# Attention, three-way MoE and squared-ReLU MoE on one core: conversion of the weights and block 1's attention listed later within block 0, and other places for block 1's keys and values

## The chip, the core and the metric

The program runs on 1 core of one Trainium2 chip. The metric is the time of one execution on the device in microseconds (us). The kernel before took 1547.14 us in the median of 3 runs (1546.5 to 1547.54).

The core's engines run side by side, each through its own list of instructions in a fixed order: PE (matmul), DVE (vector), ACT (activation), POOL (GpSimd), and SP, which here only issues DMAs. An instruction that waits holds up everything behind it on its engine.

## The reference

All inputs are float32. With B = 8 batches, H = 8 heads, S = 576 positions and D = 64, so 4608 tokens of width 512:

```
k_p, v_p = mean of k, v over groups of 8 positions        # 72 keys and values per head
attn = softmax(q @ k_p.T / sqrt(D))                       # row maximum subtracted
x = (attn @ v_p), heads side by side                      # 4608 x 512
h = max(x @ w1, x @ w2, x @ w3)                           # 4608 x 768
y = h @ w_out                                             # 4608 x 512
g = max(y @ w_in, 0);  out = (g * g) @ w_out2             # 768 and 2048 hidden columns
```

## The kernel before

**Numbers.** A float32 operand is split into a high and a low part, and each product is made of three matmuls (`PARTS`). The weights arrive as 64-bit numbers in 512 KB pieces and are converted on the chip. One conversion (`weights`, lines 128 to 164) is one DMA on SP into a tile `wraw`, two ACT instructions (L148, L149), two DVE instructions (L150, L153), the high part on ACT (`w` or `wo` from `wbits`, L121) and the low part on POOL (L122). The first stage needs 24 of them: `w_f_e` for f = 0 to 5 and e = 0 to 2, and `wo_0` to `wo_5`.

**Blocks.** The tokens go through attention and the first MoE in 12 blocks of 384 (`moe1`). Block 0 is the first 384 tokens of batch 0. Block 1 is the last 192 tokens of batch 0 and the first 192 of batch 1, so it is the first that needs the keys and values of batch 1. A block's MoE has 22 steps (`STEPS`): 18 that make `h` (one for each weight piece `w_f_e`, 12 matmuls at L465) and 4 that make `y` (18 matmuls each at L484). Attention of a block is done for four pairs of heads: load, prepare (pooled keys `ks` into `kbd`, the queries' parts `qs`), scores and softmax (`sc`, `st`, `ss`), transpose (`tr`, `pt`), values (`av`, then the pair's part of `x`, split by ACT at L121 and DVE at L122). Every matmul of a step reads all four pairs' `x`. So the steps of f = 0 begin pair by pair as `x` comes, and the steps of f = 1 start only when the fourth pair is there. Below, x0 to x3 are the four pairs of block 0.

**What sets the order.** `todo` is a list of pieces of work with a listing time in steps; `run` sorts it and calls the pieces, and a scheduler then places each instruction on its engine, in an order of its own that starts from this one. Block j's steps are listed from 22 j on; block 1's attention is listed from about ten steps before block 0's first step on; conversion i (0 to 23) is listed at 0.9 i - 12 (lines 505 to 508).

**Places.** The raw tiles of this stage (`wraw`, the keys `kr`, the values `vr`) take four places in turn (`place`). Six tiles `spare0` to `spare5` have the places in which `wo_0` to `wo_5` are kept later; until then block 0's own loads use them once: `kq` (keys and queries of a pair, four tiles) and `natural` (three tiles, the values of batch 0, pooled by matmuls `vp` at L250). These are seven loads, so the last `kq` takes one of the four raw places. All DMAs that matter here are issued by SP, in its order.

Of the kernel before, what the change touches and what calls it, by code (L numbers as in the profile page):

```python
# [10 lines left out]
F32 = mybir.dt.float32  # L11
# [9 lines left out]
P = 128  # L21
B, H, S, D = 8, 8, 576, 64
POOL = 8
SP = S // POOL
NPAIR = H // 2
NT = B * S
DM = H * D
KD = DM // P
FF1 = 768
KF1 = FF1 // P  # L30
FF2 = 2048
KF2 = FF2 // P
NE = 3
# [11 lines left out]
STEPS = NE * KF1 + KD  # L45

LEAD_LOAD, LEAD_PREP, LAG_T, LAG_V, LEAD_X = 10, 4, 3, 3, 4

# [32 lines left out]
def attention_moe_kernel(ctx: ExitStack, tc: tile.TileContext, q, k, v, vn, w1, w2, w3, wo1, wi2, wo2, out):  # L85
# [27 lines left out]
    def place(kind):  # L113
        if shared[0]:
            turns["both"] += 1
            return f"raw{turns['both'] % 4}"
        turns[kind] += 1
        return f"raw{2 * kind + turns[kind] % 2}"
# [56 lines left out]
    raw_p = s_at.enter_context(tc.tile_pool(name="raw_p", bufs=4, side="right"))  # L175
# [23 lines left out]


    spare = [f"spare{i}" for i in range(KF1)]
    unused = list(spare)

    def early(shape, name):
        if unused:
            return w_p.tile(shape, F32, tag=unused.pop(0), name=name)
        return raw_p.tile(shape, F32, tag=place(1), name=name, bufs=1)

    def load_k(b, p):
        kr = raw_p.tile([P, 2 * 512], F32, tag=place(1), name="kr", bufs=1)[:, :S]  # L210
        nc.sync.dma_start(out=kr, in_=k[b, p])
        return kr

    def load_v(b, p):
        vr = raw_p.tile([P, 2, D, POOL], F32, tag=place(1), name="vr", bufs=1)[:SP]
        nc.sync.dma_start(out=vr, in_=v[b - NATURAL, :, 2 * p : 2 * p + 2])
        return vr

# [12 lines left out]
    def load_natural(b):  # L231

        tiles = []
        for s0 in range(0, S, 2 * P):
            t = early([P, 2, DM], "natural") if b == 0 else raw_p.tile([P, 2, DM], F32, tag=place(1), name="natural", bufs=1)
            n = min(2 * P, S - s0)
            if n == 2 * P:
                nc.sync.dma_start(out=t, in_=vn[b, s0 : s0 + n].rearrange("(a p) d -> p a d", p=P))
            else:
                nc.sync.dma_start(out=t[:n, 0], in_=vn[b, s0 : s0 + n])  # L240
            tiles.append(t)
        return tiles

    def pool_v(tiles):
        vp = mm_ps.tile([P, 512], F32, tag="ps", name="vp")[:SP]
        last = (S - 1) // P
        for i in range(last + 1):
            n = min(P, S - i * P)
            c = MID - i * P // POOL
            nc.tensor.matmul(  # L250
                vp, lhsT=sums[:n, c : c + SP], rhs=tiles[i // 2][:n, i % 2], start=(i == 0), stop=(i == last)
            )
        for h in range(2):
            vh = vp.rearrange("s (p h d) -> s h p d", h=2, d=D)[:, h]
            split_scaled(vst[:, :, 2 * h], vst[:, :, 3 + 2 * h], vh, V_SCALE)
# [3 lines left out]
    def pieces(j):  # L259

        t = 0
        while t < T1:
            b, s0 = divmod(j * T1 + t, S)
            n = min(T1 - t, S - s0)
            yield b, s0, n, t
            t += n

    def score_tiles(n):
        m = P if n % P == 0 else n // 2
        return [(c, m) for c in range(0, n, m)]  # L270

    def attention(j):

        x_t[j] = [None] * NPAIR
        n_tiles = sum(NPAIR * len(score_tiles(n)) for _, _, n, _ in pieces(j))
        pace = (STEPS - 1) / n_tiles
        at = (j - 1) * STEPS + pace / 2 - (LAG_T + LAG_V + LEAD_X)
        for b, s0, n, t in pieces(j):
            if s0 == 0 and b < NATURAL:
                tiles = []  # L280
                when = at - pace / 2 + LAG_T + LAG_V if t else at + pace / 2
                todo.append((when - LEAD_LOAD, lambda b=b, tiles=tiles: tiles.extend(load_natural(b))))
                todo.append((when, lambda tiles=tiles: pool_v(tiles)))
            for p in range(NPAIR):
                load, prepare, softmax, transpose, values = attend(j, b, s0, n, p, t)
                todo.append((at - LEAD_LOAD, load))
                todo.append((at - LEAD_PREP, prepare))
                tiles = score_tiles(n)
                if j < LIGHT:
                    todo.append((at, functools.partial(softmax, tiles)))  # L290
                for c, m in tiles:
                    if j >= LIGHT:
                        todo.append((at, functools.partial(softmax, [(c, m)])))
                    todo.append((at + LAG_T, functools.partial(transpose, c, m)))
                    at += pace
                todo.append((at - pace + LAG_T + LAG_V, values))

    used = []

# [7 lines left out]
    def attend(j, b, s0, n, p, t):  # L307
# [4 lines left out]
        def load():  # L312
            if j == 0:
                kq = early([P, 2 * 512], "kq")
                kr.append(kq[:, :S])
                qr.append(kq[:, S : S + n])
                nc.sync.dma_start(out=kr[0], in_=k[b, p])
            elif first:
                kr.append(load_k(b, p))
            if j:  # L320
                qr.append(raw_p.tile([P, T1], F32, tag="qr", name="qr", bufs=2)[:, :n])
            nc.sync.dma_start(out=qr[0], in_=q[b, p, :, s0 : s0 + n])
            if first and b >= NATURAL:
                vr.append(load_v(b, p))
# [177 lines left out]

    todo = []
    attention(0)
    for f in range(KF1):
        for e in range(NE):
            todo.append((0.9 * (NE * f + e) - 12, functools.partial(load_w1, f, e)))
    for kk in range(KF1):
        todo.append((0.9 * (NE * KF1 + kk) - 12, functools.partial(load_wo1, kk)))
    for j in range(NB1 - 1):  # L510
        add_moe1(j)
        attention(j + 1)
# [10 lines left out]
    for i, (src, raw, prepare) in enumerate(second):  # L523
        when = STEPS * (SECOND[0] + (i + 0.5) * (SECOND[1] - SECOND[0]) / len(second))
# [53 lines left out]
    early = [functools.partial(load_y, 0, r) for r in range(2)] + [functools.partial(mix_y, 0)]  # L578
# [150 lines left out]
```

## Time and profile before

| | us |
|---|---|
| median of 3 runs | 1547.14 |
| the profiled execution | 1546.39 |
| its span | 1544.7 |
| PE busy | 1509.4 |
| DVE busy | 948.2 |
| ACT busy | 623.5 |
| POOL busy | 199.4 |

The profiled execution took 1546.39 us, and its span, from the first to the last recorded instruction, is 1544.7 us. PE is busy for 98% of it. The page cuts the span into 40 slices; only in the first three is PE's busy share below nine tenths, and only in the first two is the granted clock at 7 tenths. So the rows of the profile that follow look at the first 127 us, in which block 0 is done.

### The profile page before, as it was taken

The numbers are of one execution on the slowest core, as the hardware profiler recorded it, in microseconds if no ns is written. First come the engines' busy times: TensorE is split into PE (matmuls) and PEld (weight loads), VectorE is DVE, ScalarE is ACT, GpSimd is POOL, SyncE is SP. The second block draws the span as 40 slices with busy tenths as digits, with TensorE's granted clock in tenths as the row PEclk, the third lists the DMA queues.
The fourth block names the chain that finished last, engine by engine and source line by source line (L and its number), as shares of the span: only waits on it lengthen the run. The fifth ranks groups of instructions, "written<-read, shape, count | busy, mean of one in ns | idle before, by whom it ended". The sixth has DMA issues, their size and how long they took to land.

```text
span 1544.7 us, 25098 instructions
## 1 busy us (share of the span) xinstructions
PE 1509.4 (98%) x9290; PEld 1413.8 (92%) x9290; DVE 948.2 (61%) x1991; ACT 623.5 (40%) x1772; POOL 199.4 (13%) x303
## 2 busy tenths in 40 slices
PE   6899999999999999999999999999999999999998
PEld 4789999999999999999999898988989888999987
DVE  6895678776776767755427555455655546464544
ACT  7875566656666556654212212121212112121211
POOL 5541122222222121322000000000000000000000
PEclk7799999999999999999999999999999999999999
DMA  7552234434334332323475424333333433343331
GB/s 226 159 172 68 76 105 149 145 95 143 122 119 143 97 132 99 102 77 123 135 289 208 150 109 164 110 121 123 112 137 124 150 123 108 111 150 109 137 109 69
DMA packets 80858, 200.87 MB, mean 130 GB/s; under 512 B 9024, under 2 KB 32576, under 8 KB 80736
## 3 DMA queue, kind: packets, MB, share of 16 engines
q1 hardware_dynamic: 73824, 189.83, 36.1%
q10 hardware_dynamic: 6912, 9.44, 1.7%
q8 instruction: 74, 1.21, 0.3%
q14 instruction: 48, 0.39, 0.1%
HBM read 157.29 MB, written 41.94 MB: 129 GB/s over the span
## 4 chain that ended last, share of the span: by engine, by line
PE 85%; DVE 5%; DMA 5%; ACT 2%; issue 2%; SPq 0%; POOL 0%; DVEq 0%; ACTq 0%; POOLq 0%
PE ps L465 25%; PE acc L645 25%; PE ps L600 21%; PE ps L484 9%; PE sc L344 2%; DMA out_dram<-o 2%; PE tr L370 2%; DMA wraw<-in_w_dram 1%; PE av L396 1%; PE av L395 1%; DVE wbits L153 1%; DMA vr<-in_v_dram 1%; DMA wraw<-in_wo_dram 1%; DMA kq<-in_k_dram 1%; DVE wbits L150 0%
## 5 line engine op out<-in xcount | busy, mean ns | idle before, releaser
L465 PE MATMUL ps<-x,w 128*128 128x384 f32 x2592 | 507.6, 343 | 1.8 <-DVE x L122 1.0
L465 PEld LDWEIGHTS ps<-x,w 128*128 128x128 f32 x2592 | 451.1, 191 | 3.9 <-DVE x L122 2.0
L645 PE MATMUL acc<-wo2s,g 128*128 128x512 f32 x1728 | 412.5, 391 | 0.0
L600 PEld LDWEIGHTS ps<-y,wi2s 128*128 128x128 f32 x3024 | 370.4, 188 | 12.5 <-PE ps L600 3.4
L600 PE MATMUL ps<-y,wi2s 128*128 128x256 f32 x3024 | 376.8, 280 | 2.8 <-DVE s L629 2.2
L645 PEld LDWEIGHTS acc<-wo2s,g 128*128 128x128 f32 x1728 | 316.2, 188 | 62.6
L121 ACT ACTIVATE g<-c 128x512 fp32r<-128x512 f32 x144 | 90.8, 630 | 410.4 <-DVE c L611 403.6
L617 DVE TENSOR_TENSOR s<-ps,s 128x512 f32<-128x512 f32 x72 | 49.8, 692 | 262.2 <-PE ps L600 261.6
L484 PE MATMUL ps<-h,wo 128*128 128x384 f32 x864 | 165.2, 339 | 0.5 <-DVE hm L473 0.4
L484 PEld LDWEIGHTS ps<-h,wo 128*128 128x128 f32 x864 | 148.9, 188 | 1.3 <-DVE hm L473 0.7
L617 DVE TENSOR_TENSOR c<-ps,s 128x512 f32<-128x512 f32 x144 | 99.0, 688 | 24.9 <-PE ps L600 21.7
L355 POOL TENSOR_TENSOR ss<-ss,st 128x144 f32<-128x144 f32 (+3 forms) x144 | 74.2, 517 | 308.7 <-DVE st L354 238.6
L473 DVE TENSOR_TENSOR hm<-ps,hm 128x384 f32<-128x384 f32 x144 | 79.5, 552 | 54.2 <-PE ps L465 50.3
L349 ACT ACTIVATE ss<-sc,st 128x72 f32<-128x72 f32 (+1 forms) x320 | 98.3, 314 | 33.3 <-DVE st L346 30.8
L122 DVE TENSOR_TENSOR g<-c,g 128x512 fp32r<-128x512 f32 x144 | 98.8, 686 | 17.3 <-ACT g L121 16.4
L611 DVE SCALAR_TENSOR_TENSOR c<-c 128x512 f32<-128x512 f32 x144 | 99.0, 688 | 2.2
L373 DVE TENSOR_TENSOR pt<-tr,pt 72x256 fp32r<-72x256 f32 (+1 forms) x160 | 61.5, 387 | 52.6 <-ACT pt L372 51.2
L344 PEld LDWEIGHTS sc<-kbd,qs 128*128 128x128 f32 (+1 forms) x480 | 73.3, 191 | 12.3 <-issue 5.3
L344 PE MATMUL sc<-kbd,qs 128*128 128x144 f32 (+1 forms) x480 | 73.9, 269 | 9.2 <-ACT kbd L195 5.3
L372 ACT ACTIVATE pt<-tr 72x256 fp32r<-72x256 f32 (+1 forms) x160 | 56.4, 355 | 58.9 <-PE tr L370 57.4
L370 PE MATMUL tr<-ident,ss 128*72 128x128 f32 (+1 forms) x320 | 59.2, 271 | 13.9 <-DVE pt L373 8.8
L349 ACT ACTIVATION_READ_ACCUMULATOR ss<-sc,st 128x1 f32 (+1 forms) x320 | 63.4, 198 | 0.0
(78 smaller groups left out, 1247.0 us busy)
## 6 DMA issues: line engine op xcount, KB each, us to landing
wo2s<-wo_dram SPq DMA_DIRECT2D x144, 512.0 KB
wi2s<-wi_dram SPq DMA_DIRECT2D x24, 512.0 KB
wraw<-in_wo_dram SPq DMA_DIRECT2D x22, 512.0 KB
wraw<-in_w_dram SPq DMA_DIRECT2D x18, 512.0 KB
y_dram<-ys ACTq DMA_DIRECT2D x48, 192.0 KB
out_dram<-o SPq DMA_DIRECT2D x36, 256.0 KB
wraw<-in_wi_dram SPq DMA_DIRECT2D x16, 512.0 KB
wi_dram<-wraw SPq DMA_DIRECT2D x16, 512.0 KB
```

The source lines that it names most:

```text
L121: nc.scalar.activation(hi, src, AF.Copy)
L122: engine.tensor_tensor(out=lo, in0=src, in1=as_f32(hi), op=ALU.subtract)
L344: nc.tensor.matmul(src[:, i], lhsT=lhsT, rhs=kbd[:, p, l], start=(n == 0), stop=(n == 2))
L349: nc.scalar.activation(ss[:, i, h], src[:, i, h], AF.Exp, bias=st[:, 0, i, h : h + 1], accum_out=st[:, 1, i, h : h + 1],)
L370: nc.tensor.transpose(tr[:, h, :m], sms[c][:, h], ident[:m, :m])
L465: nc.tensor.matmul(ps, lhsT=w1_t[f, e][:, a, kk * P : (kk + 1) * P], rhs=x[kk][:, c], start=(n == 0), stop=(n == 3 * KD - 1),)
L473: nc.vector.tensor_tensor(out=hm, in0=ps, in1=hm, op=ALU.max)
L484: nc.tensor.matmul(ps, lhsT=wo1_t[kk][:, a, d * P : (d + 1) * P], rhs=hs[kk][:, c], start=(n == 0), stop=(n == 3 * KF1 - 1),)
L600: nc.tensor.matmul(bank[:, u * HT : (u + 1) * HT], lhsT=wi2_t[2 * gr + u][i][:, a, o + kk * P : o + (kk + 1) * P], rhs=y_t[j][m][:, c, kk] ...
L611: nc.vector.scalar_tensor_tensor(out=c, in0=c, scalar=0.0, in1=c, op0=ALU.max, op1=ALU.mult)
L617: nc.vector.tensor_tensor(out=c, in0=bank, in1=other, op=ALU.add)
L645: nc.tensor.matmul(acc_t[j][2 * half + i], lhsT=g[:, a, u * HT + i * P : u * HT + (i + 1) * P], rhs=wo2_t[j, 4 * gr + 2 * u + h][:, c], st ...
```

## The change

Three things are changed. The conversions are listed five steps later, at 0.9 i - 7. Block 1's attention is listed from eight steps later on and more closely, so that it ends where it did (`rate` scales its pace and its leads by 14/22). And the list `unused` of places that `early` gives out has the four places `spare2` to `spare5` two times more, with `early` now asked by `load_k`, `load_v` and all of `load_natural`. So the last `kq` of block 0 and seven of the eight loads of batch 1's keys and values take those places; the eighth, and all later ones, take a raw place as before.

```
+LATE = 8
+CONVERT, CONVERT_PACE = -7, 0.9
...
     spare = [f"spare{i}" for i in range(KF1)]
-    unused = list(spare)
+    unused = spare + 2 * spare[2:]
...
     def load_k(b, p):
-        kr = raw_p.tile([P, 2 * 512], F32, tag=place(1), name="kr", bufs=1)[:, :S]
+        kr = early([P, 2 * 512], "kr")[:, :S]
...
     def load_v(b, p):
-        vr = raw_p.tile([P, 2, D, POOL], F32, tag=place(1), name="vr", bufs=1)[:SP]
+        vr = early([P, 2, D, POOL], "vr")[:SP]
...
-            t = early([P, 2, DM], "natural") if b == 0 else raw_p.tile([P, 2, DM], F32, tag=place(1), name="natural", bufs=1)
+            t = early([P, 2, DM], "natural")
...
         at = (j - 1) * STEPS + pace / 2 - (LAG_T + LAG_V + LEAD_X)
+        rate = 1 - LATE / STEPS if j == 1 else 1
+        at, pace = at + LATE if j == 1 else at, pace * rate
...
-                when = at - pace / 2 + LAG_T + LAG_V if t else at + pace / 2
+                when = at - pace / 2 + rate * (LAG_T + LAG_V) if t else at + pace / 2
...
-                todo.append((at - LEAD_LOAD, load))
-                todo.append((at - LEAD_PREP, prepare))
+                todo.append((at - rate * LEAD_LOAD, load))
+                todo.append((at - rate * LEAD_PREP, prepare))
...
-                    todo.append((at + LAG_T, functools.partial(transpose, c, m)))
+                    todo.append((at + rate * LAG_T, functools.partial(transpose, c, m)))
...
-                todo.append((at - pace + LAG_T + LAG_V, values))
+                todo.append((at - pace + rate * (LAG_T + LAG_V), values))
...
-            todo.append((0.9 * (NE * f + e) - 12, functools.partial(load_w1, f, e)))
+            todo.append((CONVERT_PACE * (NE * f + e) + CONVERT, functools.partial(load_w1, f, e)))
...
-        todo.append((0.9 * (NE * KF1 + kk) - 12, functools.partial(load_wo1, kk)))
+        todo.append((CONVERT_PACE * (NE * KF1 + kk) + CONVERT, functools.partial(load_wo1, kk)))
```

On SP, the queue that issues the loads, the place right after the third pair's keys. A `vr` or `kr` is a load for batch 1, a `wraw` a piece of weights, `qr` block 1's queries. Before:

```order
L317 DMA kq<-in_k_dram 128x576
L322 DMA kq<-in_q_dram 128x384
L317 DMA kq<-in_k_dram 128x576
L322 DMA kq<-in_q_dram 128x384
L322 DMA qr<-in_q_dram 128x192 x2
L133 DMA wraw<-in_w_dram 128x1024 x3
L211 DMA kr<-in_k_dram 128x576
L133 DMA wraw<-in_w_dram 128x1024
L216 DMA vr<-in_v_dram 72x1024
```

And in the changed kernel, from the third pair's keys to the fourth's:

```order
L323 DMA kq<-in_k_dram 128x576
L328 DMA kq<-in_q_dram 128x384
L328 DMA qr<-in_q_dram 128x192
L137 DMA wraw<-in_w_dram 128x1024 x2
L328 DMA qr<-in_q_dram 128x192
L137 DMA wraw<-in_w_dram 128x1024 x2
L220 DMA vr<-in_v_dram 72x1024
L215 DMA kr<-in_k_dram 128x576
L323 DMA kq<-in_k_dram 128x576
L328 DMA kq<-in_q_dram 128x384
L137 DMA wraw<-in_w_dram 128x1024
```

Four loads of weights, one of values and one of keys have moved ahead of the fourth pair's `kq`. That load now waits for PE to have read the `natural` tile whose place it takes.

On ACT, the place at which the fourth pair's `x` of block 0 is split, after the third pair's (`av_423` before, `av_402` after). `w_2_1` and the like are the high parts of the weights. Before:

```order
L148 ACTIVATE wbits<-wraw 128x512
L149 ACTIVATE wraw<-wraw 128x512
L121 ACTIVATE w_2_1_570<-wbits 128x512
L372 ACTIVATE pt<-tr 72x2x128
L349 ACTIVATE ss,st<-sc,st 96x72 x4
L121 ACTIVATE w_2_2_588<-wbits 128x512
L121 ACTIVATE w_3_0_615<-wbits 128x512
L121 ACTIVATE qs<-qr 128x192
L372 ACTIVATE pt<-tr 72x2x96
L349 ACTIVATE ss,st<-sc,st 96x72 x4
L121 ACTIVATE x<-av_561 128x384
```

And in the changed kernel:

```order
L199 ACTIVATE kbd<-ks 64x72 x2
L378 ACTIVATE pt<-tr 72x2x128
L355 ACTIVATE ss,st<-sc,st 96x72 x4
L153 ACTIVATE wraw<-wraw 128x512
L152 ACTIVATE wbits<-wraw 128x512
L153 ACTIVATE wraw<-wraw 128x512
L152 ACTIVATE wbits<-wraw 128x512
L125 ACTIVATE w_4_0_762<-wbits 128x512
L125 ACTIVATE qs<-qr 128x192
L125 ACTIVATE x<-av_446 128x384
```

Ahead of the fourth pair's `x` stood ten finished conversions (to `w_3_0`); now there are 13 (to `w_4_0`). Of block 1's softmax, four calls of L349 over 96 rows stood ahead of it, and now three.

## Rows read from the trace of the kernel before

**Rows 1.** PE, PEld, DVE, ACT, POOL busy (us); granted clock; DMA; by stretch.

```profile
0.00:66.50 66.50, 45.51 (x190) 34.44 (x191) 48.27 (x97) 50.91 (x181) 38.05 (x43) 0.74 0.62 196
66.50:126.85 60.35, 56.75 (x337) 53.84 (x336) 54.92 (x120) 44.36 (x137) 25.78 (x23) 0.97 0.50 160
126.85:200.00 73.15, 73.15 (x447) 72.44 (x447) 43.19 (x115) 37.38 (x121) 9.20 (x18) 1.00 0.23 67
```

**Rows 2.** PE in order of time: start, duration, idle time before it, releaser.

```profile
61.78 1.59 PE L385 MATMUL av<-pt,vst 72*128 72x192 f32 x6
63.17 2.18 PE L465 MATMUL ps<-x,w 128*128 128x384 f32 x6
...
101.90 0.36 PE L395 MATMUL av<-pt,vst 72*128 72x192 f32 x1 [2.09 <-DVE xf L399]
```

**Rows 3.** The view of Rows 1 in three shorter stretches.

```profile
49.00:59.50 10.50, 7.28 (x44) 5.28 (x43) 8.31 (x18) 9.77 (x34) 6.10 (x6) 0.99 0.63 216
59.50:66.00 6.50, 6.49 (x27) 5.86 (x28) 6.43 (x12) 6.50 (x22) 4.44 (x7) 0.50 0.30 90
99.00:104.00 5.00, 2.78 (x19) 2.21 (x17) 4.94 (x8) 3.03 (x8) 3.37 (x3) 0.98 0.38 127
```

**Rows 4.** ACT in order of time: first and fourth x, one conversion.

```profile
31.81 0.49 ACT L121 ACTIVATE x<-av 128x384 fp32r<-128x384 f32 x1
...
53.56 0.65 ACT L148 ACTIVATE wbits<-wraw 128x512 f32<-128x512 f32 x1
54.12 0.67 ACT L149 ACTIVATE wraw<-wraw 128x512 int32<-128x512 uint32 x1
54.70 0.61 ACT L121 ACTIVATE w<-wbits 128x512 fp32r<-128x512 f32 x1
55.22 0.36 ACT L372 ACTIVATE pt<-tr 72x256 fp32r<-72x256 f32 x1
55.48 0.30 ACT L349 ACTIVATE ss<-sc,st 96x72 f32<-96x72 f32 x1
...
59.36 0.48 ACT L121 ACTIVATE x<-av 128x384 fp32r<-128x384 f32 x1
```

**Rows 5.** The view of Rows 1 from 14 to 59.8 us.

```profile
14.00:59.80 45.80, 30.73 (x144) 24.61 (x143) 36.90 (x77) 38.20 (x136) 27.40 (x25) 0.70 0.60 191
```

**Rows 6.** ACT's waits from 14 to 66 us: total, times, longest.

```profile
ACT wbits L148 <- DMA wraw<-in_w_dram: 2.2, 2, 1.5
ACT w L121 <- DVE wbits L153: 2.2, 1, 2.2
ACT kbd L195 <- DVE ks L221: 1.5, 1, 1.5
```

**Rows 7.** DVE in order of time: values of batch 1, and long instructions.

```profile
42.17 1.22 DVE L228 TENSOR_REDUCE vs<-vr 72x128 f32<-72x1024 f32 x1 [2.21 <-DMA vr<-in_v_dram]
...
64.04 3.57 DVE L150 SCALAR_TENSOR_TENSOR wbits<-wbits,wraw 128x512 int32<-128x512 int32 x2
...
76.90 1.21 DVE L228 TENSOR_REDUCE vs<-vr 72x128 f32<-72x1024 f32 x1
```

**Rows 8.** ACT: the first high part of wo.

```profile
92.80 0.63 ACT L121 ACTIVATE wo<-wbits 128x512 fp32r<-128x512 f32 x1
```

**Rows 9.** DMA issues of SP in order of time.

```profile
6.20 0.74 SPq L317 DMA_DIRECT2D kq<-in_k_dram  x1
...
11.15 1.60 SPq L133 DMA_DIRECT2D wraw<-in_w_dram  x3
```

**Rows 10.** The pooling matmuls on PE.

```profile
8.36 6.27 PE L250 MATMUL vp<-natural,sums 128*72 128x512 f32 x10
```

**Rows 11.** POOL: the low part of the third pair's queries.

```profile
14.52 1.00 POOL L122 TENSOR_TENSOR qs<-kq,qs 128x384 fp32r<-128x384 f32 x1
```

**Rows 12.** The chain of waits: two loads, start and time to landing.

```profile
4.44 7.97 DMA kq<-in_k_dram
...
29.09 4.62 DMA wraw<-in_w_dram
```

## The prediction

> **What bounds the kernel now.** I read the page's slices first, then the busy times by stretch, PE's timeline and waits, and last ACT's and DVE's rows in the first 127 us. The reader is to see that from 126.85 us on PE has no gap (73.15 of 73.15 us up to 200 us) and the granted clock is 1.00 [rows 1]. PE's matmuls are the same before and after, so an end of block 0 that comes earlier by some time ends the kernel earlier by that time, as long as block 1 keeps PE full. What there is to win lies in two stretches. Up to 66.5 us PE is busy for 45.5 us at a mean clock of 0.74. From 66.5 to 126.85 us it idles 60.35 - 56.75 = 3.6 us, and its mean clock of 0.97 means that 6% of the stretch, 3.6 us, ran at half speed, which costs 1.8 us: 5.4 us in all [rows 1].
>
> The border at 66.5 us is set by x3, the fourth pair's part of x. ACT splits x0 at 31.8 and x3 at 59.4 us, done at 59.8 [rows 4]. PE then ends the last matmuls of f = 0 at 63.17 + 2.18 = 65.35 us [rows 2], 5.5 us after x3, all at half clock (0.50 from 59.5 to 66 us, with PE busy throughout [rows 3]). In the second stretch the largest single gap is one of 2.09 us before 101.90 us, and PE waits there for DVE's `xf` [rows 2]; DVE is busy for 4.94 of the 5 us from 99 to 104 us [rows 3]. So the first stretch hangs on the chain of softmax over ACT, DVE, POOL and PE, the second on PE with a backlog of DVE.
>
> **The change part by part.** *ACT's queue ahead of x3.* Although the conversions are listed later, they stand earlier on ACT, since the keys and values of batch 1 no longer take the four raw places in turn with them. Counting ACT's order from 14 us (behind the third pair's `kbd`) to x3, the changed kernel has 5 L148, 4 L149 and 3 high parts more, 2 `kbd` more, and 4 exponentials and one `pt` fewer. From start to start these take 0.56 us (53.56 to 54.12), 0.58, 0.52 and, for a `pt`, 0.26 us; an exponential takes 0.30 [rows 4], and for a `kbd` I take the 0.26 of `pt`. That is 2.8 + 2.3 + 1.6 + 0.5 - 1.2 - 0.3 = 5.7 us more ahead of x3.
>
> *ACT's waits.* In these 45.8 us ACT is busy for 38.2 [rows 5], so it idles 7.6. Of this 2.2 us is for weights that had not landed, 2.2 for DVE's half of a conversion, and 1.5 for pooled keys [rows 6]: 5.9 us. The second is DVE stopped at 40 to 42.17 us by values of batch 1 that were still in flight [rows 7]. The new places remove what causes the first two, since loads of keys and values no longer wait for a conversion to free their place, nor weights for keys and values; the third belongs to the fourth pair's `kbd`, whose place in the queue is now behind other work. I take all 5.9 us as gone and the other 1.7 as left: x3 at 14 + 38.2 + 5.7 + 1.7 = 59.6 us, 0.2 earlier than before. The bounds are no idle at all (57.9) and the whole 7.6 us left (65.5).
>
> *What PE has done by then.* Up to the end of f = 0 the order has 6 `sc`, 2 `tr` and 6 `av` matmuls of block 1 fewer on PE. The six `av` stood behind x3 at half clock and took 1.59 us [rows 2]; they no longer do, so f = 0 ends 1.6 us sooner after x3. Later they are made up at full clock: 0.8 us for the `av`, and for the eight others, of like size, 1.1: 1.9 us added. By the end of block 1 the counts are equal (135 `sc` for 136, 84 `tr` for 82).
>
> *The stretch after f = 0.* By x3, 13 conversions are done in place of 10. So three fewer are left to DVE, ACT and POOL, in the stretch in which DVE was full. This can give back between nothing and the whole 5.4 us. I take the one gap that DVE alone made, 2.1 us, and the 1.8 us of half clock, of which I see no cause other than that gap: 3.9 us.
>
> *The places.* `wo_2` to `wo_5` now wait for the last reader of keys and values in their places. DVE pools the last values but one at 76.9 us [rows 7], and the first high part of `wo` is written at 92.8 [rows 8]. The cost is nothing, and would be something only if those reads came 16 us later.
>
> *The fourth pair's load.* It was issued at 6.20 us, ahead of the weights (11.15) [rows 9]. Now it takes the place of a `natural` tile, waits for the pooling on PE, which ends at 8.36 + 6.27 = 14.6 us [rows 10], and stands on SP behind four weights, a `vr` and a `kr` that waits for the third pair's queries on POOL (15.5 us [rows 11]). So it is issued at about 15.6 to 16.3 us. It lands 4.6 us later by the nearest row of a load in this stretch, or 8.0 by the longest [rows 12]: 20.9 to 24.3. ACT reaches its queries behind 4 conversions' first halves, 2 high parts, 12 exponentials, 3 `pt` and 2 `vst`, 14 + 10.5 = 24.5 us. So I cost it at nothing, 0.2 us from the point at which ACT, and all behind it, would wait; everything else of pair 3 has more than 30 us up to x3.
>
> **The sum.** -0.2 (x3) - 1.6 (`av` behind it) + 1.9 (the same work later) - 3.9 (stretch after) = -3.8 us. The profiled execution took 1546.39 us, of which 1544.7 are span, and becomes 1542.6; it was 0.75 us faster than the median of 1547.14, and that becomes 1543.3.
>
> The clock is where the Trainium skill speaks against the change. The rows: at 49 to 59.5 us PE was busy for 7.28 of 10.5 us at clock 0.99, and then fell to 0.50 for 6.5 us in which it never idled [rows 3]. The Trainium skill, "TensorE: Matmul & The Clock Gate", section "HAM oscillation", says that a PE with idle gaps is throttled and begins the next work cold. The trace agrees. By that rule a PE with 14 matmuls fewer to fill its gaps ahead of x3 could fall to 1.2 GHz more, and 6.5 us more of it behind x3 would cost 3.3 us, most of the gain.
>
> A second one is on DVE. At 64.04 us two L150 took 3.57 us, though a whole conversion step is near 0.6 us on ACT [rows 4, 7]. The Trainium skill, "SBUF — State Buffer", section "Who interferes with whom", has a DVE instruction with two SBUF inputs and a GpSimd instruction lock each other out. The rows fit it. By that rule three more low parts ahead of x3, each some 1 us or more on POOL as the queries' in [rows 11], would hold DVE and x3 by up to 3 us: a sum of about -0.8.
>
> **The rivals.** *The later stretch keeps its loss.* The gap at 101.9 us hangs on DVE's order, not on its load alone: `xf` has one buffer, and PE waits for it wherever long DVE work stands ahead. Then, or where the two rules above hold, x3 comes as forecast or a little later and 3.9 us is not returned: -0.2 - 1.6 + 1.9 = +0.1, 1547.2. For it: the gap's releaser. Against it: three conversions fewer on a full DVE.
>
> *A larger gain.* ACT never idles, x3 at 57.9 (-1.9), and the clock is full behind it: the 5.5 - 1.6 = 3.9 us to the end of f = 0 become 2.0 and that end is 5.4 us earlier. With +1.9 and all 5.4 returned: -8.9, 1538.2. For it: the new loads are early. Against it: the softmax chain has waits of its own.
>
> *The conversions stand in x's way (slower).* ACT is in order, so 5.7 us of weights not yet needed stand ahead of x3. If the 7.6 us of idle time stays, because the waits were the softmax chain's and only bore other names, x3 comes at 65.5 us (+5.7), with -1.6 + 1.9 and half of the 5.4 returned: +3.3, 1550.4. It decides against the kernel from x3 at about 65 us on. For it: in-order engines often trade one wait for another. Against it: three named waits, of 5.9 us, have their cause removed.
>
> **How the numbers follow.** The forecast (-2 to -6 us) has 0.47, the kept loss 0.23, the larger gain 0.12, slower 0.18. A change of 0.2%, 3.1 us, is about what a measurement of this kernel can tell from none. The forecast lies beyond it in seven parts of ten: 0.33, with the larger gain 0.45 faster. The rest of the forecast and the kept loss make 0.37. Slower by more than that is 0.18. The range runs from the larger gain, 1538, to just short of the slower rival, 1550. The likeliest case's own is 1541 to 1545.
>
> **What would show it.** Right: ACT's waits for `wraw` and `wbits` before x3 near zero; x3 at 58 to 61 us with `w_4_0` converted; steps of f = 1 from about 64 us; no gap of 2 us on PE near 100 us; block 1's steps from about 123 us. Wrong: ACT waiting for the fourth pair's queries near 24 us, x3 behind 63 us, or PE at half clock far behind f = 0.

## The result: slower, by 0.54%

The changed kernel took 1554.7 us in the median of 6 runs (1553.86 to 1558.76), the kernel before 1546.91 us beside it: a ratio of 1.0054, with an interval of 1.0041 to 1.0067, about 8 us slower. Forecast were 1543.3 us and a range of 1538 to 1550. Both the sign and the range were missed.

| | before | after |
|---|---|---|
| profiled execution, span (us) | 1546.39, 1544.7 | 1553.86, 1552.1 |
| x0, x3 on ACT (us) | 31.81, 59.36 | 29.94, 69.43 |
| first step of block 1 on PE (us) | 126.69 | 131.63 |
| halves of the conversions on DVE, 14 to 127 us (48 of each kernel) | 40.4 us | 47.0 us |

Lines of the changed kernel have numbers 4 to 6 higher than before: L157 is the second half of a conversion on DVE (L153 before), L154 the first (L150), L125 and L126 the high and low parts (L121 and L122), L200 the low part of `kbd`.

First the stretches, which answer to [rows 1] (PE, PEld, DVE, ACT and POOL busy, granted clock, DMA):

```profile
0.00:66.50 66.50, 37.14 (x144) 27.47 (x144) 55.02 (x90) 46.91 (x156) 34.55 (x39) 0.72 0.68 212
66.50:126.85 60.35, 57.91 (x350) 56.33 (x348) 52.78 (x112) 45.20 (x144) 29.13 (x24) 0.92 0.43 133
126.85:200.00 73.15, 73.15 (x450) 72.46 (x449) 44.23 (x120) 38.60 (x130) 6.96 (x16) 1.00 0.22 68
76.70:131.60 54.90, 54.67 (x341) 53.86 (x340) 45.25 (x104) 37.83 (x122) 22.88 (x20) 0.97 0.39 121
```

Up to 66.5 us PE is busy for 37.1 us where it was 45.5, and DVE for 55.0 where it was 48.3. The later stretch is as full as forecast: from 76.7 us to the start of block 1 PE idles 0.2 us. It only begins ten microseconds late. On ACT, in order of time, the first, second and fourth part of x answer to [rows 4], and on PE the end of f = 0 and the first step of block 1 answer to [rows 2]:

```profile
29.94 0.47 ACT L125 ACTIVATE x<-av 128x384 fp32r<-128x384 f32 x1
52.31 0.47 ACT L125 ACTIVATE x<-av 128x384 fp32r<-128x384 f32 x1
...
69.43 0.46 ACT L125 ACTIVATE x<-av 128x384 fp32r<-128x384 f32 x1
```

```profile
69.94 1.33 PE L471 MATMUL ps<-x,w 128*128 128x384 f32 x3 [1.47 <-ACT x L125]
72.01 2.29 PE L471 MATMUL ps<-x,w 128*128 128x384 f32 x6 [0.74 <-DVE x L126]
...
76.78 4.82 PE L471 MATMUL ps<-x,w 128*128 128x384 f32 x18
...
131.63 2.31 PE L471 MATMUL ps<-x,w 128*128 128x384 f32 x12
```

x0 is 1.9 us earlier than before, x3 10.1 us later. From x0 to x1 it takes 22.4 us. What stands there is read from PE's, ACT's and SP's waits, 14 to 75 us (14 to 69.5 for ACT), as in [rows 6] (total, times, longest); for PE and SP the same wait in the kernel before stands first:

```profile
PE tr L370 <- DVE pt L373: 6.8, 4, 3.6
...
PE tr L376 <- DVE pt L379: 15.3, 5, 6.4
...
PE av L391 <- ACT pt L378: 3.9, 2, 2.0
```

```profile
ACT wraw L153 <- DMA wraw<-in_w_dram: 6.2, 5, 2.6
ACT w L125 <- DVE wbits L157: 2.9, 1, 2.9
```

```profile
SPq L133 <- DVE wbits L153: 6.8, 7, 2.2
...
SPq L137 <- DVE wbits L157: 37.2, 14, 5.5
```

PE waits for DVE's `pt`, ACT for weights that have not landed, and the loads of these weights wait on SP for DVE, which has not finished with the place. All three end at DVE. PE's total for `pt` more than doubled, and SP's for the halves went from 6.8 to 37.2 us. On DVE itself, in order of time, with POOL beside it:

```profile
46.84 0.44 DVE L352 TENSOR_REDUCE st<-sc 96x4 f32<-96x288 f32 x1
47.21 3.56 DVE L157 SCALAR_TENSOR_TENSOR wbits<-wraw,wbits 128x512 int32<-128x512 int32 x1
50.69 1.13 DVE L200 SCALAR_TENSOR_TENSOR kbd<-ks,kbd 64x72 fp32r<-64x72 f32 x3
...
58.05 0.68 DVE L154 SCALAR_TENSOR_TENSOR wbits<-wbits,wraw 128x512 int32<-128x512 int32 x1
58.76 3.52 DVE L157 SCALAR_TENSOR_TENSOR wbits<-wraw,wbits 128x512 int32<-128x512 int32 x1
62.20 0.41 DVE L379 TENSOR_TENSOR pt<-tr,pt 72x256 fp32r<-72x256 f32 x1
```

```profile
46.69 1.08 POOL L361 TENSOR_TENSOR ss<-ss,st 96x288 f32<-96x288 f32 x1 [1.38 <-DVE st L360]
47.74 2.48 POOL L126 TENSOR_TENSOR w<-wbits,w 128x512 fp32r<-128x512 f32 x2
50.17 1.04 POOL L126 TENSOR_TENSOR qs<-qr,qs 128x192 fp32r<-128x192 f32 x1
...
58.30 0.96 POOL L361 TENSOR_TENSOR ss<-ss,st 96x288 f32<-96x288 f32 x1 [4.53 <-ACT w L125]
59.22 2.51 POOL L126 TENSOR_TENSOR w<-wbits,w 128x512 fp32r<-128x512 f32 x2
```

A half that takes 0.68 us elsewhere takes 3.5 us when it starts during one POOL instruction that has two others behind it; it ends some 0.6 us after the last of those two. The `pt` at 62.20 us, for which PE waits, stands behind such a half. Adding up over DVE's groups from 14 to 127 us (before, then after; busy, mean ns of one, idle time before them):

```profile
L150 DVE SCALAR_TENSOR_TENSOR wbits<-wbits,wraw 128x512 int32<-128x512 int32 x24 | 21.7, 913 | 1.2 <-ACT wraw L149 0.9 <-issue 0.2
L153 DVE SCALAR_TENSOR_TENSOR wbits<-wraw,wbits 128x512 int32<-128x512 int32 x24 | 18.7, 784 | 0.1
L196 DVE SCALAR_TENSOR_TENSOR kbd<-ks,kbd 64x72 fp32r<-64x72 f32 x17 | 6.1, 356 | 0.3
```

```profile
L157 DVE SCALAR_TENSOR_TENSOR wbits<-wraw,wbits 128x512 int32<-128x512 int32 x24 | 27.7, 1157 | 0.3
L154 DVE SCALAR_TENSOR_TENSOR wbits<-wbits,wraw 128x512 int32<-128x512 int32 x24 | 19.3, 815 | 2.0 <-ACT wraw L153 1.5 <-ACT wbits L152 0.4
L200 DVE SCALAR_TENSOR_TENSOR kbd<-ks,kbd 64x72 fp32r<-64x72 f32 x15 | 8.7, 580 | 0.3
```

The same 48 halves take 6.6 us longer, and two `kbd` fewer take 2.6 us longer. Below, "excess" is an estimate: the time of DVE instructions above their length when nothing holds them (0.61 us per half in a row of them plus 0.08, 0.20 and 0.06 for `kbd`, 0.16 for the small additions to `st`, 0.3 to 0.5 for low parts of x and queries), worked out from every DVE row of a stretch and good to a few microseconds. "DVE idle" is the sum of the idle times in the same rows.

Of the 7.4 us of span, 4.9 are there at block 1's first step (126.69 to 131.63 us). At block 7's first step the kernels are still 5.15 us apart (488.82 and 493.97 us), at block 8's 6.80 (553.83 and 560.63 us). Between them lies a gap that both kernels have (before, then after; columns as above). It is 0.4 us more of idle time, and a mean clock of 0.91 in place of 0.96: 10% more of the 40 us at half clock, which is worth up to 2 us.

```profile
480.00:520.00 40.00, 37.83 (x226) 36.51 (x225) 28.06 (x82) 26.56 (x93) 10.20 (x19) 0.96 0.40 128
```

```profile
480.00:520.00 40.00, 37.43 (x222) 36.57 (x221) 29.18 (x85) 25.66 (x91) 10.15 (x19) 0.91 0.42 137
```

When the second MoE begins, the two are 6.4 us apart (784.56 and 790.93 us). Most of the rest is one wait of PE for DVE's `s` in that stage, which the kernel before does not have at this place; behind it the two are 7.4 us apart:

```profile
1389.28 3.07 PE L606 MATMUL ps<-y,wi2s 128*128 128x256 f32 x24 [1.02 <-DVE s L635]
```

### The profile page after: what moved, and what is told of

It is laid out like the page before. It is cut to its first block, busy times and chain, and to the rows that moved or that the text cites. A ratio compares the mean times of both kernels' runs of the same rounds, so it can differ in the third digit from the quotient of the medians.

```text
span 1552.1 us, 25079 instructions
## 1 busy us (share of the span) xinstructions
PE 1508.1 (97%) x9290; PEld 1415.7 (91%) x9290; DVE 956.5 (62%) x1991; ACT 624.3 (40%) x1772; POOL 199.8 (13%) x303
## 4 chain that ended last, share of the span: by engine, by line
PE 84%; DVE 6%; DMA 5%; ACT 2%; issue 2%; SPq 0%; POOL 0%; DVEq 0%; ACTq 0%; POOLq 0%
PE ps L471 25%; PE acc L651 24%; PE ps L606 21%; PE ps L490 9%; PE sc L350 2%; DMA out_dram<-o 2%; PE tr L376 2%; DMA wraw<-in_wo_dram 1%; DVE wbits L157 1%; PE av L401 1%; PE av L402 1%; DMA wraw<-in_w_dram 1%; ACT ss L355 1%; DVE wbits L154 1%; DMA kq<-in_k_dram 0%
## 5 line engine op out<-in xcount | busy, mean ns | idle before, releaser
L651 PEld LDWEIGHTS acc<-wo2s,g 128*128 128x128 f32 x1728 | 316.3, 188 | 62.6
L125 ACT ACTIVATE g<-c 128x512 fp32r<-128x512 f32 x144 | 90.8, 631 | 411.3 <-DVE c L617 404.3
L126 DVE TENSOR_TENSOR g<-c,g 128x512 fp32r<-128x512 f32 x144 | 98.6, 685 | 17.4 <-ACT g L125 16.5
L350 PEld LDWEIGHTS sc<-kbd,qs 128*128 128x128 f32 (+1 forms) x480 | 73.9, 191 | 13.9 <-issue 5.1
L376 PE MATMUL tr<-ident,ss 128*72 128x128 f32 (+1 forms) x320 | 60.1, 272 | 17.3 <-DVE pt L379 17.1
L125 ACT ACTIVATE h<-hm 128x384 fp32r<-128x384 f32 x72 | 37.7, 524 | 71.3 <-DVE hm L479 70.8
```

The source lines that it names most:

```text
L125: nc.scalar.activation(hi, src, AF.Copy)
L126: engine.tensor_tensor(out=lo, in0=src, in1=as_f32(hi), op=ALU.subtract)
L350: nc.tensor.matmul(src[:, i], lhsT=lhsT, rhs=kbd[:, p, l], start=(n == 0), stop=(n == 2))
L376: nc.tensor.transpose(tr[:, h, :m], sms[c][:, h], ident[:m, :m])
L651: nc.tensor.matmul(acc_t[j][2 * half + i], lhsT=g[:, a, u * HT + i * P : u * HT + (i + 1) * P], rhs=wo2_t[j, 4 * gr + 2 * u + h][:, c], st ...
```

## The experiments

Two theories stood against each other. "Lock": DVE's instructions with two inputs in SBUF are held while POOL reads, and the change brings more of them together with POOL. "Queue": ten more halves (30 instead of 20) stand ahead of x3 on DVE, and that alone is the delay. Each part of the change was also run by itself. The ratio is to the kernel before on the same chip. The last four columns are of one profiled execution each, in us: x3 is its low part on DVE, block 1 its first step on PE.

| kernel | median us | ratio (95%) | x3 | block 1 | excess, 14 to 127 us | DVE idle |
|---|---|---|---|---|---|---|
| before | 1546.4 to 1547.0 | 1 | 61.2 | 126.7 | 15.1 | 13.0 |
| after | 1554.7 | 1.0054 (1.0041 to 1.0067) | 71.4 | 131.6 | 22.5 | 7.4 |
| e1 after, POOL only writes | 1541.69 | 0.9967 (0.9956 to 0.9978) | 64.7 | 121.8 | 6.6 | 19.9 |
| e2 before, POOL only writes | 1541.81 | 0.9969 (0.9960 to 0.9979) | 59.2 | 120.2 | 5.9 | 21.2 |
| e3 places only | 1551.25 | 1.0028 (1.0017 to 1.0039) | 69.7 | 131.9 | 19.1 | 10.8 |
| e4 places, conversions later | 1552.92 | 1.0038 (1.0023 to 1.0053) | 59.4 | 131.6 | 22.9 | 5.6 |
| e9 both listings later, old places | 1548.52 | 1.0007 (0.9996 to 1.0018) | 62.2 | 127.6 | 13.9 | 14.6 |
| e5 after, low parts on DVE | 1545.22 | 0.9998 (0.9989 to 1.0007) | 65.5 | 122.5 | 7.7 | 5.5 |
| e10 before, low parts on DVE | 1549.18 | 1.0017 (1.0007 to 1.0026) | 67.0 | 127.4 | 4.8 | 11.9 |
| e6 after, 15 through a bank | 1536.70 | 0.9938 (0.9926 to 0.9951) | 58.4 | 120.2 | 10.3 | 14.0 |
| e7 before, 10 through a bank | 1553.15 | 1.0042 (1.0029 to 1.0054) | 62.6 | 129.4 | 12.5 | 18.4 |
| e8 after, bank of `av` | 1559.17 | 1.0081 (1.0067 to 1.0095) | 62.5 | 134.9 | 11.5 | 19.1 |
| e11 after, 24 through a bank | 1539.57 | 0.9952 (0.9939 to 0.9964) | 57.0 | 126.5 | 8.6 | 11.7 |
| e12 e6, queries' low parts on DVE | 1547.73 | 1.0002 (0.9994 to 1.0011) | 60.9 | 124.0 | 13.2 | 8.9 |

The column on block 1 shows what a kernel wins or loses in the stage that was changed. Behind it each kernel also meets the gap at 480 to 520 us or not: e6 and e11 do not have it (40.00 of 40 us busy at clock 1.00), e3 hardly (39.46), the others have 2.1 to 2.6 us of idle time and a clock of 0.91 or 0.96 there.

### POOL writes but does not read (e1, e2)

```
-        engine.tensor_tensor(out=lo, in0=src, in1=as_f32(hi), op=ALU.subtract)
+        if write_only:      # the weights of the first MoE
+            engine.tensor_tensor(out=lo[:, :1], in0=src[:, :1], in1=as_f32(hi)[:, :1], op=ALU.subtract)
+            for _ in range(2):
+                engine.memset(as_f32(lo), 0.0)
+            return
```

> The changed kernel, but GpSimd's low part of a stage-1 weight is one column of the subtraction and then two fills of the whole tile with zeros, of about the same length on GpSimd, which write and do not read (so the weights' low parts are left out of the result). 16 and 16 halves of a conversion stand ahead of x3 on DVE (15 and 15 in the changed kernel). Theory 'lock' (DVE's two-input instructions are held while GpSimd reads; in the changed kernel the instructions of DVE up to x3 hold 16.5 us above their shortest times, against 6.8 before): single halves of 3.5 us vanish, the excess falls under 6 us, x3 on DVE at 58 to 63 us in place of 71.4, time 1543 to 1549. Rival 'queue' (the ten more halves ahead of x3 are themselves the delay, the locks fall into time that DVE would wait anyway): x3 still at 68 to 74, time 1552 to 1558.

> The same edit on the kernel before (the weights' low parts are left out of the result), which keeps its 10 and 10 halves ahead of x3. Theory 'lock': at most 6.8 us of excess to win and 8 us of idle time on DVE to hide it: x3 on DVE 2 to 5 us earlier than 61.2, time 1542 to 1546. Rival 'queue': x3 within 1 us of 61.2, time 1546 to 1548.

The changed kernel drops by 13 us, to 1541.69, and the kernel before by 5, to 1541.81. Both are below the ranges of either theory, by 1.3 and 0.2 us. With POOL writing (but for one column), the change makes no difference to the time. At block 1's first step it still does, 121.8 us against 120.2; e2 loses that again in the later gap (clock 0.91, e1 0.96), so the equal times are in part luck. POOL was not relieved: its work on the 18 `w` takes 18.5 + 6.9 = 25.4 us (25.2 us in the changed kernel).

```profile
L129 POOL MEMSET w<- 128x512 f32 x36 | 18.5, 525 | 1.3
...
L127 POOL TENSOR_TENSOR w<-wbits,w 128x1 fp32r<-128x1 f32 x18 | 6.9, 385 | 22.1 <-ACT w L125 22.0
```

The same halves on DVE of e1:

```profile
L159 DVE SCALAR_TENSOR_TENSOR wbits<-wbits,wraw 128x512 int32<-128x512 int32 x24 | 16.9, 712 | 4.2 <-ACT wraw L158 3.5 <-ACT wbits L157 0.6
L162 DVE SCALAR_TENSOR_TENSOR wbits<-wraw,wbits 128x512 int32<-128x512 int32 x24 | 16.7, 701 | 0.2
```

They fall from 47.0 to 33.6 us. x3 comes 6.8 us earlier with 32 halves ahead of it, two more than in the changed kernel; "queue" expected 68 to 74. It is not back at 61: "lock" had 58 to 63, so some of the delay is the queue's. One reserve: the scheduler places a fill otherwise than a subtraction, so e1's order is not exactly that of the changed kernel.

### One part at a time (e3, e4, e9)

The edits are the constants of the change set back: e3 has `LATE = 0` and `CONVERT = -12`, e4 has `LATE = 0`, and e9 has

```
-    unused = spare + 2 * spare[2:]
+    unused = list(spare)
```

with keys, values and `natural` of batch 1 in the four raw places, as before.

> Only the places are changed; conversions and block 1's attention are listed as before. 15 and 15 halves ahead of x3 on DVE and 14 high parts on ACT. Theory 'conversions ahead of x3' (lock and queue together): like the changed kernel or worse, x3 on DVE at 70 to 75, time 1553 to 1558. Rival 'listing of block 1' (the later, denser attention of block 1 is what costs): 1546 to 1549.

> Places changed and conversions listed later, block 1's attention listed as before (no LATE). 10 and 10 halves ahead of x3 on DVE and 10 high parts on ACT, as before the change. Theory 'conversions ahead of x3': x3 on DVE back to 58 to 63 us, time 1541 to 1549. Rival 'places' (the new places of the fourth pair's queries and of batch 1's keys and values delay x1 to x3 by themselves): x3 at 67 or later, time 1551 to 1557.

> Conversions and block 1's attention listed later as in the changed kernel, but with the old places. 11 conversions, 21 halves ahead of x3 on DVE. If the places are what lets conversions crowd ahead of x3 and fills DVE (places alone took 1551.3, places with later conversions 1552.9), this is 1544 to 1549 with 10 us or more of idle time and 13 to 18 us of excess on DVE at 14 to 127 us. Rival 'the later listing costs by itself': 1551 to 1556.

The places alone make the kernel slower, the later listing alone changes nothing beyond the interval. e3's time lies between the ranges of theory and rival, yet it starts block 1 at 131.9 us, as late as the changed kernel (131.6). Its profiled execution ends 5.4 us sooner (1548.48 and 1553.86 us) for the gap near 500 us that it hardly has. So the part that I had costed at nothing is the one that costs. Not by a wait for a place: with the new places DVE has 5.6 to 10.8 us of idle time and 19.1 to 22.9 us of excess, with the old ones 13.0 to 14.6 and 13.9 to 15.1.

e4 refuted half of what I expected of it. With 20 halves ahead of x3, x3 is back at 59.4 us, as "queue" and "lock" both say, and yet the kernel is 6 us slower than before. PE's rows show where it went:

```profile
110.03 0.36 PE L376 MATMUL tr<-ident,ss 96*72 96x96 f32 x2 [1.31 <-DVE xf L405]
116.60 2.18 PE L490 MATMUL ps<-h,wo 128*128 128x384 f32 x9 [1.17 <-ACT wo L125]
121.50 1.33 PE L490 MATMUL ps<-h,wo 128*128 128x384 f32 x6 [2.18 <-ACT wo L125]
```

The output weights come too late: the conversions not done ahead of x3 were still owed, by a DVE with 22.9 us of excess. PE is busy for 52.56 of the 61 us from 66 to 127 (57.4 before). Neither the place of x3 nor the count of conversions ahead of it decides alone: what is not converted ahead of x3 is converted behind it, under the same holds.

### The low part on DVE (e5, e10)

```
-        split(w, convert(raw_pool, load_raw(raw_pool, src)), nc.gpsimd)
+        split(w, convert(raw_pool, load_raw(raw_pool, src)))
```

> The changed kernel with the low part of a stage-1 weight on DVE in place of GpSimd: 24 two-input subtractions of about 0.61 us more on DVE (14.6 us up to 127 us), against a kernel whose DVE holds 22.5 us above the shortest times in that stretch. Theory 'lock': the excess falls to 5 to 8 us, as in the two fill kernels (6.6 and 5.9), so DVE's total stays about where it was: time 1549 to 1556, no more than 1 us above the changed kernel for all that added work. Rival 'queue' (work on DVE is what counts, holds are not): 14.6 us more on an engine that is full, time 1562 to 1570.

> The kernel before with the low part of a stage-1 weight on DVE. Its DVE had 13.0 us idle and 15.1 us of excess at 14 to 127 us; the work added is 24 x 0.71 = 17.1 us. Theory 'a hold costs as much as work': excess falls by about 9 to 6 and 8 us of the added work lands on a DVE that waits 13: 1545 to 1550. Rival 'holds in the kernel before are hidden in its waits': the added work is not paid for, 1552 to 1557.

Nothing is left out here. DVE gets 17.1 us of work more in e5, and the kernel becomes about 9 us faster than the changed one, below the range of either theory. DVE's busy time from 14 to 127 us, which I had taken for the measure, even rises, from 103.1 to 104.7 us; so a microsecond held cost more than one of work. That the low parts stand in an order laid out for them, while a hold strikes whatever comes next, is my reading, and not tested. DVE's groups in e5:

```profile
L157 DVE SCALAR_TENSOR_TENSOR wbits<-wraw,wbits 128x512 int32<-128x512 int32 x24 | 17.3, 721 | 0.1
L154 DVE SCALAR_TENSOR_TENSOR wbits<-wbits,wraw 128x512 int32<-128x512 int32 x24 | 16.6, 697 | 1.0 <-ACT wbits L152 0.6 <-ACT wraw L153 0.4
L126 DVE TENSOR_TENSOR w<-wbits,w 128x512 fp32r<-128x512 f32 x18 | 13.1, 727 | 0.0
```

The halves are at their shortest, and x3 comes at 65.5 us with 29 halves and 14 low parts ahead of it on DVE. From 66 to 127 us PE is busy for 60.92 of 61 us, at clock 1.00. The kernel before, with less excess to lose, gets 0.17% slower by the same edit, inside the range expected. Between the two, the change now makes the kernel faster: 0.9998 against 1.0017, about 3 us, and 4.9 us at block 1's first step (122.5 against 127.4). The size is near what I had forecast, the way is not: x3 comes at 65.5 us, and the gain is in the full stretch behind it.

### One input from PSUM (e6, e7, e8, e11, e12)

```
+        b = a if bank is None else bank      # bank: mm_ps.tile([P, 512], I32, tag="ps")
-        nc.scalar.activation(as_f32(a), as_f32(high), AF.Abs, scale=REBIAS)
+        nc.scalar.activation(as_f32(b), as_f32(high), AF.Abs, scale=REBIAS)
...
-            out=a, in0=a, scalar=3, in1=low, ...
+            out=b, in0=b, scalar=3, in1=low, ...
...
-            out=a, in0=high, scalar=-0x80000000, in1=a, ...
+            out=a, in0=high, scalar=-0x80000000, in1=b, ...
```

> The changed kernel with the middle value of the first 15 conversions (wbits between ACT and DVE) in a PSUM bank of the matmuls' own pool instead of SBUF: both DVE halves then have one SBUF input and one from PSUM; GpSimd's work and the results stay as they are. 11 conversions ahead of x3. Theory 'lock' (only two SBUF inputs are held): no half above 0.8 us among the first 15 conversions, excess on DVE at 14 to 127 us 10 to 14 us instead of 22.5, time 1543 to 1549. Rival 'GpSimd slows DVE whatever it reads': halves of 1.5 to 3.5 us remain, time 1551 to 1556.

> The same on the kernel before, for its first 10 conversions; 13 conversions stand ahead of x3. Theory 'lock': excess on DVE at 14 to 127 us 9 to 13 instead of 15.1, time 1542 to 1547. Rival 'GpSimd slows DVE whatever it reads', and 13 conversions ahead of x3 in place of 10: 1548 to 1553.

> As the kernel with the matmuls' bank, but the bank is that of the second half of `av` (block 0's transposes then all use the one bank of their own, so the softmax chain has one bank less). 11 conversions ahead of x3. Theory 'lock': no half above 0.8 us among the first 15 conversions, time 1543 to 1550; the transposes' single bank may cost 1 to 3 us of that. Rival: as for the other bank, 1551 to 1557.

> The changed kernel with all 24 conversions through the matmuls' banks (15 before). Theory 'lock': the excess of the last nine conversions (2.9 us) goes as well, but the bank is then asked for by the running steps too: 1535 to 1540. Rival 'the steps' banks are needed': steps of block 0 wait for a bank, 1540 to 1548.

> As the kernel with 15 conversions through the matmuls' banks, and the low part of the queries of blocks 0 and 1 on DVE in place of GpSimd (0.30 to 0.55 us each on DVE). Its remaining excess is 10.3 us at 14 to 127 us, 4.9 of it on `kbd`. Theory 'lock': the excess falls by 2 to 5 us for about 6 us of work: 1535 to 1541, no gain to speak of. Rival: DVE waits enough (14 us) to hide it, 1531 to 1535.

POOL's work stays as it is; only where DVE reads one operand differs. For DVE in e6, count and shortest, median and longest duration in ns; then its groups of the nine conversions that kept two SBUF inputs:

```profile
L155 DVE SCALAR_TENSOR_TENSOR bank<-bank,wraw x15: 679/690/700, 15.8 to 73.7; 128x512 int32<-128x512 int32 x15
L158 DVE SCALAR_TENSOR_TENSOR wbits<-wraw,bank x15: 652/673/689, 16.5 to 75.6; 128x512 int32<-128x512 int32 x15
```

```profile
L155 DVE SCALAR_TENSOR_TENSOR wbits<-wbits,wraw 128x512 int32<-128x512 int32 x9 | 8.3, 928 | 1.2 <-POOL ss L368 1.0 <-ACT wbits L153 0.2
L158 DVE SCALAR_TENSOR_TENSOR wbits<-wraw,wbits 128x512 int32<-128x512 int32 x9 | 6.8, 760 | 0.1
```

None of the 30 halves with an operand in PSUM takes over 0.70 us, nor do the 128 in e7, e8, e11 and e12. In the changed kernel the longest second half took 3.56:

```profile
L157 DVE SCALAR_TENSOR_TENSOR wbits<-wraw,wbits x24: 675/686/3562, 16.7 to 115.9; 128x512 int32<-128x512 int32 x24
```

This refutes the rival that POOL slows DVE whatever DVE reads. The changed kernel itself says the same: its 27 low parts `pt`, which read one operand from PSUM, take 0.42 us at most up to 127 us. e6 takes 1536.7 us, below its range, and beats both kernels, the kernel before by 0.62% (0.49 to 0.74). 6.5 us of that are there at block 1's first step (120.2 us); part of them is order, since 22 halves stand ahead of its x3, where the changed kernel has 30. The rest is later: it has no gap at 480 to 520 us, where PE (the first number behind the length) is busy for 40 of 40 us. That stretch in e6:

```profile
480.00:520.00 40.00, 40.00 (x250) 39.71 (x249) 29.69 (x80) 25.25 (x83) 7.98 (x17) 1.00 0.40 135
```

e11's time (1539.6 us) is within its range, but not for the reason given. Its block 1 starts at 126.5 us, no earlier than before: PE is busy for 55.7 of the 61 us from 66 to 127 (58.0 in e6) and waits 1.5 us for conversions' halves (0.2 in e6), as the rival said. What it gains, it gains where the gap near 500 us is missing.

The other three did not come out. In e7, too, no half with an operand in PSUM takes over 0.70 us, and it took 1553 us: x3 is at 62.6 us behind 13 conversions, and later PE waits once for 3.8 us, for DVE's `hm`:

```profile
106.00 1.55 PE L472 MATMUL ps<-x,w 128*128 128x384 f32 x4 [3.79 <-DVE hm L480]
```

Whether the banks that the conversions take from the matmuls cost e7 time stays open.

e8 has one bank less for the transposes and block 1's `av`. PE waits for DVE's and ACT's `pt` for 14.1 us up to 70 us (9.6 in e6), and from 66 to 127 us it idles 7.4 us (3.0 in e6); I had put the bank at 1 to 3 us. Of the 22 us between the two, 14.7 are there at block 1's first step (134.9 against 120.2 us), and 7.0 between the first steps of blocks 7 and 8, where the gap lies (59.6 us in e6, 66.6 in e8). PE's waits in e8, up to 70 us:

```profile
PE tr L383 <- DVE pt L386: 10.3, 5, 3.5
PE av L398 <- ACT pt L385: 3.8, 4, 2.7
```

e12 lost what e6 had won. The queries' subtractions moved to DVE have two SBUF inputs themselves and are held (about 5 us of excess on them and their like), and excess is 13.2 instead of 10.3 us. x3 is 2.5 us later than in e6, and the gap at 480 to 520 us is back (37.42 of 40 us busy at clock 0.91): from block 7's first step to block 8's it takes 67.2 us, 7.6 more than e6, and that is most of the 11 us between the two. Why that gap comes and goes stays open. So a low excess does not ensure a fast kernel: the order around it counts for as much in e7, e8 and e12.

## Why the prediction was wrong

**ACT's queue ahead of x3.** The count of work was right: 15 first halves on ACT and 13 high parts stand ahead of x3, and ACT was busy for 44.4 us from 14 us to the end of x3's split, where I had 38.2 + 5.7 = 43.9. It idled 11.5 us where I had left 1.7. The failed step is that this sum was made on ACT alone. The same conversions put ten more halves on DVE, 6.1 us, and the sum has no term for them. DVE up to x3: 59.4 us busy after, 43.0 before; 6.1 of the 16.4 us are the ten halves, some 9.7 are excess (16.5 against 6.8), and 6.2 us of idle time went. That makes x3 10.2 us later. In the kernel before DVE had that idle time, so ACT looked like the chain; the change took it away.

**ACT's waits.** I took 5.9 us as gone, since their causes were removed. The causes were, the waits were not: weights 2.2 before and 6.2 us after, DVE's half 2.2 and 2.9. The load now waits for DVE to free the place, not for a key to land.

**The places.** The waits that I looked for, of `wo` for its place and of the fourth pair's load, did not appear: its `kq` was issued at 16.0 and 16.5 us, and ACT split its queries at 25.6 us without waiting. But the places are the part that costs (e3, e9), by what they let happen on DVE and POOL.

**The shared port.** The Trainium skill, "SBUF — State Buffer", section "Who interferes with whom", has a DVE instruction with two SBUF inputs contend with a GpSimd instruction that reads SBUF, but not with one that only writes. It has a DVE instruction with at most one SBUF input, outside the modes in which it uses two ports, not contend at all. For the conversions the runs agree: means of 815 and 1157 ns beside reading, 712 and 701 beside mostly writing (e1), 0.70 us at most with one input in PSUM (e6). The additions to `st` have a single SBUF input and were held all the same: 1.58 us at 59.49 us in the kernel before, just ahead of x3, where the same shape mostly takes 0.15 to 0.18. Whether they run in such a mode no run shows. I had named the rule and priced it at 3 us, as three more low parts of 1 us. The mis-sized term is this one: the excess up to x3 grew by some 9.7 us, since a held half waits through a row of POOL's instructions, and since not three but all low parts meet a DVE that no longer pauses.

**What PE has done, and the stretch after.** Both came out. f = 0 ends 4.4 us after x3 (69.9 to 74.3; 5.5 before), where I had 3.9. From the start of f = 1 to block 1 it takes 54.9 us in place of 60.2; the forecast was 2 us less than before (3.9 returned, 1.9 added), the measured gain is 5.3. It came behind an x3 10 us late.

**The clock.** The mean granted clock from 66.5 to 126.85 us fell from 0.97 to 0.92, because f = 0 now reaches 10 us into this stretch; from 76.7 us on it is 0.97. Behind x3 PE did run longer at 1.2 GHz, as the prediction feared: the clock is 0.50 from 69.8 to 79.8 us, 10 us, where it was 6.5 before. But the kernel before had it at 0.50 from 104 to 107 us as well, and the changed kernel has 1.00 from 80 us on. So the clock does not explain the loss by itself.

**The rivals.** The slower one had the sign, a time of 1550 and x3 at 65.5 us, by idle time that stays on ACT. ACT's idle time did stay, and grew, but what held ACT was DVE, which the rival does not name. It was given 0.18.

What is shown: with POOL mostly writing, the change is worth 0 in time (e1 against e2), and with the low parts on DVE it gains 3 us (e5 against e10); so the loss comes with POOL's reading beside DVE's halves. The places alone bring it (e3). What is not: why block 1 still starts 1.6 us later in e1 than in e2, how much of e6's gain is order, and why the gap near 500 us comes and goes. From block 7's first step to block 8's it takes 65.0 us before and 66.7 after, with the gap, and 59.6 in e6, without it: nearly as much as the change is worth.

## What to carry to other kernels

When work is moved ahead of a critical result, count it on every engine that it uses, not only on the one that looked like the chain; an engine at 80% with idle time between its instructions can be the next bound. Idle time of DVE that falls beside POOL's work is not free to fill: two-input instructions put there are held. Where a bound DVE has POOL reading beside it, one of DVE's two operands in PSUM takes it out of the conflict, and even giving POOL's work to DVE can pay (in e5; in e10 it did not). And a difference of a few microseconds is first placed in the run: here a gap 350 us behind the changed stage was worth 5 to 7 us by itself.

## What was not expected of the hardware

A DVE half was held not for one POOL instruction but through up to three that followed each other without a pause: 3.56 us from 47.21, beside POOL's from 46.69 to 50.22 us, for work of 0.68. POOL is held in turn: the queries' subtraction on POOL at 50.17 us took 1.04 us, the same shape 0.60 at 35.79 us. Even DVE's small additions to `st` were held, one over 128x6 elements for 1.09 us in place of 0.15 (at 39.16 us in the changed kernel), and one of the kernel before for longer:

```profile
59.49 1.58 DVE L353 TENSOR_SCALAR st<-st 96x4 f32<-96x4 f32 x1 [0.84 <-ACT ss L349]
```
